# Input product: three weight slots converted again in the second token pair instead of being completed and stored in the first

## The chip, the cores and the metric

The kernel runs on one core of a Trainium2 chip. The metric is the device time of one execution in microseconds, the median of several executions. Engines are named as the profile names them: PE (TensorE matmuls) and PEld (its weight loads), DVE (VectorE), ACT (ScalarE), POOL (GpSimd) and SP (SyncE, which here does nothing but issue DMAs, one after the other).

## The reference

Three layers run one after the other on 3072 tokens of width 512: a chunked attention with eight memory rows, a feed-forward layer with `w_in` and `w_out`, and a gated feed-forward layer after an RMS norm.

```python
x = attention(q, k, v, mem_k, mem_v)        # (4, 8, 768, 64) -> (3072, 512)
h = x @ w_in                                # w_in (512, 2048)
sp = np.where(h > 20.0, h, np.log1p(np.exp(np.minimum(h, 20.0))))
x = (h * np.tanh(sp)) @ w_out
xn = x / np.sqrt(np.mean(x * x, axis=-1, keepdims=True) + 1e-06) * rms_g
g = xn @ w_gate
out = (g / (1 + np.exp(-g)) * (xn @ w_val)) @ w_out2
```

The weights come as 64-bit floats, so the kernel has to turn them into 32-bit ones on the chip before it can multiply with them. The change touches only `h = x @ w_in`.

## The kernel before

**Tokens.** The 3072 tokens are eight blocks of 384, taken as four token pairs j = 0 to 3. Before a pair can be multiplied, its two blocks have to come out of the attention, in pieces (`att_a` to `att_e1`) that are placed between the products of the pair before. The attention's inputs are loaded two tiles of 128 tokens ahead (`kn`, `qn`, and `vw` in eight small DMAs a tile).

**The input product.** `w_in` is cut into eight keys ("i", 0) to ("i", 7) of 256 columns. Every operand is a high and a low part, so a product is six matmuls of 384 columns (lines 566 to 568). The first pair is multiplied in the plain way: `unit(b, i)` takes block b and key i with four products, 16 units in all. The other three pairs use `group1(j, i)`, a scheme with seven products for both blocks, eight groups in each pair. Its token side needs seven sums of the pair's blocks (`t_pieces`, `sum_pieces`: lines 542 to 545, then six splits at lines 140 and 141, the last thing before a pair can run), its weight side seven pieces of a key. A group leaves its four PSUM banks by ACT copies and DVE additions (lines 577 to 598 and 653).

**Weight slots.** Five slots of 1792 KB (`W_SLOT` = 0, 4, 3, 2, 1, 0, 4, 3 for keys 0 to 7) hold the eight keys in turn: keys 5, 7 and 6 come into the slots of keys 0, 1 and 2.

**Conversion.** `cv_all` is one long sequence of steps which `cv_upto` moves on between products. A key has two raw halves of 512 KB, loaded into two raw buffers in turn (`load_raw`, line 136; a new load has to wait until line 188 has read the half before last). Each half takes ACT lines 180 and 183, then DVE lines 187, 188 and 194. A plain job (`add_plain`) then splits four pieces (lines 140 on ACT and 141 on DVE), which is what `unit` needs. A pair job (`add_pair`, used for the later weights) adds four sums (two on POOL, two on DVE) and splits all seven pieces. All of a conversion's instructions on ACT and most on DVE are pinned: they keep their program order.

**Completion.** `finish(key)` makes the seven pieces from the four of a plain job: two additions on DVE that rebuild the 32-bit weights (line 254), two sums on POOL (lines 259 and 260), two on DVE (lines 261 and 262) and two splits. In the first pair keys 0, 1, 2 and 7 are completed, in the second 6, 5, 4 and 3. A key that loses its slot is stored to device memory in two halves by `w_store` (line 124, `wi<-w`): keys 0, 1 and 2 in the first pair, 7, 6 and 5 in the second. `reload` brings a key back as one load (line 119, `w<-wi`): keys 2, 1, 0 in the second pair, 5, 6, 7 in the third, 2, 1, 0 in the fourth.

**What sets the order.** `slots` hands out the work between products: attention pieces, conversion steps, `finish` steps and stores at slot numbers. The instruction order on each engine is then fixed when the program is built. Each engine runs its own list in order, and all DMAs are in the one list of SP: an instruction that waits holds back all that stand behind it on its engine.

Of the kernel before, what the change touches and what calls it, by code (L numbers as in the profile page):

```python
# [24 lines left out]
W_AT = {1: 0, 2: 1, 4: 2, 3: 3, 5: 4, 6: 5, 7: 6}  # L25
W_IN = {1: 0, 2: 1, 3: 2, 4: 3, 5: 4, 6: 5, 7: 6}
# [3 lines left out]
def tile_kernel(  # L30
# [67 lines left out]
    def store_later(dst, src):  # L98
        late.append((tick[0] + 2, dst, src))

    def flush(all_=False):
        tick[0] += 1
        while late and (all_ or late[0][0] <= tick[0]):
            _, dst, src = late.pop(0)
            nc.sync.dma_start(out=dst, in_=src)
# [6 lines left out]
    wtab, wslot = {}, {}  # L112
# [4 lines left out]
    def w_load(key, u):  # L117
        s = w_slot(u)
        nc.sync.dma_start(out=s.bitcast(F32), in_=wd[key].bitcast(F32))
        wtab[key] = as7(s)  # L120
# [28 lines left out]
    def add_pair(key, arr0, f0, arr1, f1, u, keep, store):  # L149
        jobs.append(("pair", key, [(arr0, "col", f0), (arr1, "col", f1)], u, keep, store))  # L150

    def add_plain(key, arr, f0, f1, u):
        jobs.append(("plain", key, [(arr, "col", f0), (arr, "col", f1)], u, True, False))
# [4 lines left out]
    def add_rows(keys, arr, fs, u):  # L158
        jobs.append(("rows", keys, [(arr, "row", f) for f in fs], u, True, False))
# [111 lines left out]
    def cv_upto(n):  # L271
        while cv_n[0] < n:
            next(cv[0], None)
            cv_n[0] += 1

    def need(key):
        while key not in wtab:
            cv_upto(cv_n[0] + 1)
# [223 lines left out]
    def att_list(j):  # L502

        out = []
        t0 = TPP * j
        for s in range(TPP + 4):
            for op, lag in (("e", 4), ("d", 3), ("c", 2), ("b", 1), ("a", 0)):
                t = t0 + s - lag
                if t0 <= t < t0 + TPP:
                    if op == "a" and t % SPB == 0:  # L510
                        out.append([(att_a0, t)])
                    out.append([(att_ops[op], t), (att_ops[op + "1"], t)])
        return out
# [7 lines left out]
    def t_pieces(j, x0, x1, new, dram, tab):  # L521

        return sum_pieces(j, x0[:, 0:2, :], x0[:, 2:4, :], x1[:, 0:2, :], x1[:, 2:4, :],
                          new, dram, tab)
# [34 lines left out]
    def product(at, w, t, bank_, first):  # L559
        ws = w[:, at].rearrange("p l (k f) -> p l k f", k=2)  # L560
        ps = bank_[:, 0:N]
        for kk in range(2):
            whi, wlo = ws[:, 0, kk, :], ws[:, 1, kk, :]
            xh, xl = t[:, 0, kk, :], t[:, 1, kk, :]
            more = dict(skip_group_check=not first)
            nc.tensor.matmul(ps, whi, xh, start=first and kk == 0, stop=False, **more)  # L566
            nc.tensor.matmul(ps, whi, xl, start=False, stop=False, **more)  # L567
            nc.tensor.matmul(ps, wlo, xh, start=False, stop=kk == 1, **more)  # L568
# [41 lines left out]
    def unit(b, i):  # L610
        need(("i", i))
        w = wtab["i", i]
        g = gp.tile([128, 2, N], F32, tag="g", name="g")
        for e in range(2):
            ps = bk[(2 * n_unit[0] + e) % 4]
            for half in range(2):
                product(2 * e + half, w, xtab[b, half], ps, half == 0)
                if half:
                    nc.scalar.copy(g[:, e, :], ps[:, 0:N])
                    if e:  # L620
                        store_later(
                            g_d[0, 2 * i:2 * i + 2, :, b, :].rearrange("f p n -> p f n"), g
                        )
                yield
        n_unit[0] += 1

    def run(parts, between):
        while parts:
            for part in list(parts):
                if next(part, "end") == "end":  # L630
                    parts.remove(part)
                else:
                    between()
# [3 lines left out]
    def group_banks(of):  # L637
        g = n_group[0]
        n_group[0] += 1
        return [bk[(4 * g + i) % of] for i in range(4)]  # L640
# [4 lines left out]
    def group1_parts(j, i):  # L645
        need(("i", i))
        g = [gp.tile([128, 2, N], F32, tag="g", name="g") for _ in range(2)]
        ts = {p: ttab_x[j, p] for p in ORDER}
        mul = lambda p, bank_, first: product(W_IN[p], wtab["i", i], ts[p], bank_, first)
        banks = group_banks(4)  # L650
        c11 = banks[0][:, 0:N]
        yield from group(mul, banks, N, g[0][:, 1, :], g[1][:, 0, :], g[1][:, 1, :])
        nc.scalar.copy(g[0][:, 0, :], c11)
        for e in range(2):
            store_later(g_d[j, 2 * i + e], g[e])
# [21 lines left out]
    class Feed:  # L677
# [24 lines left out]
        def next(self, s):  # L702
            self.load(s + 3)
            self.split(s + 3)
            self.load(s + 5)
            return self.out.pop(0)
# [100 lines left out]
    W_SLOT = (0, 4, 3, 2, 1, 0, 4, 3)  # L807
    up = list(range(F1 // 2))
    down = up[::-1]
    for i in (0, 1, 2, 3, 4, 5, 7, 6):  # L810
        add_plain(("i", i), w_in, 2 * i, 2 * i + 1, W_SLOT[i])
    for f, u in zip(range(0, F1, 3), (5, 6, 7, 1, 2, 3)):
        fs = range(f, min(f + 3, F1))
        add_rows([("o1", x) for x in fs], w_out, fs, u)
# [16 lines left out]
    first = att_list(0)  # L831
# [25 lines left out]
    def slots(pieces, conv, tail=(), more={}, cap=10 ** 6):  # L857


        state = dict(n=0, att=0, tail=0)  # L860
        plist, n_slots = pieces
        first_cv, to = conv
        base = cv_n[0]

        def between():
            state["n"] += 1
            n = state["n"]
            flush()
            if n in more:
                more[n]()  # L870
            span = n_slots - 7
            while state["att"] < len(plist) and state["att"] * span < n * len(plist):
                for fn, t in plist[state["att"]]:
                    fn(t)
                state["att"] += 1
            if n > first_cv:
                cv_upto(min(cap, base + (to - base) * (n - first_cv) // (n_slots - first_cv)))
            if n >= n_slots - 7 and tail:
                if state["tail"] == 0:
                    state["t"] = tail()  # L880
                    for fn in state["t"][0]:
                        fn()
                elif state["tail"] <= len(state["t"][1]):
                    state["t"][1][state["tail"] - 1]()
                state["tail"] += 1

        return between

    def tail_of(j):
        return lambda: t_pieces(j, xb.pop(2 * j), xb.pop(2 * j + 1), t_new, None, ttab_x)  # L890

    def keep_w(i, half):
        return lambda: w_store(("i", i), half)

    def reload(pos, seq):
        if pos < 3:
            w_load(("i", seq[5 + pos]), W_SLOT[seq[5 + pos]])

    CV_I = 64

    def then(more, n, fn):
        more.setdefault(n, []).append(fn)

    def finish_at(more, i, n):
        part = finish(("i", i))
        for step in range(3):
            then(more, n + step, lambda: next(part))

    def calls(more):
        return {n: (lambda fns=fns: [fn() for fn in fns]) for n, fns in more.items()}  # L910
# [2 lines left out]
    units += [(b, i) for i in (2, 3, 4, 5, 7, 6) if i >= NHEAD for b in range(2)]  # L913
    at = {u: 4 * n + 4 for n, u in enumerate(units)}
    more = {}
    for i in range(3):
        finish_at(more, i, at[1, i] + 1)
        for half in range(2):
            then(more, at[1, i] + 4 + 3 * half, keep_w(i, half))
    finish_at(more, 7, at[1, 7] + 1)  # L920
    bt = slots((att_list(1), 4 * len(units)), (0, 73), tail_of(1), calls(more), CV_I)
    for b, i in units:
        run([unit(b, i)], bt)
    more = {}
    for i, ns in ((7, (3, 5)), (6, (9, 12)), (5, (16, 19))):
        for half, n in enumerate(ns):
            then(more, n, keep_w(i, half))
    for n, i in enumerate((6, 5, 4, 3)):
        finish_at(more, i, 7 * n + 1)
    bt = slots((att_list(2), 56), (0, 0), tail_of(2), calls(more))  # L930
    for pos, i in enumerate(down):
        group1(1, i, bt)
        reload(pos, down)
    bt = slots((att_list(3), 56), (0, 0), tail_of(3))
    for pos, i in enumerate(up):
        group1(2, i, bt)
        reload(pos, up)
    att_stack.close()
    w2p[0] = ctx.enter_context(
        tc.tile_pool(name="w2p", bufs=1, side="right", reuse_waits="tile")  # L940
    )
    bt = slots(([], 56), (0, CV_I + 64))
# [26 lines left out]
    for s, (m, i) in enumerate(steps):  # L969
# [3 lines left out]
        if i == F1 // 2 - 1 and m < NB - 1:  # L973
            assert not pend
            n = order[m]
# [54 lines left out]
    bt = between2(CV_I + 196, 140)  # L1030
# [29 lines left out]
    bt = between2(CV_I + 262, 125)  # L1060
# [53 lines left out]
```

## Time and profile before

| | us |
|---|---|
| median of 3 runs | 1208.36 (1205.7 to 1210.33) |
| profiled execution | 1208.05 |
| its span, first to last instruction | 1206.3 |
| PE busy | 1164.7 (97%) |
| DVE busy | 820.8 (68%) |
| ACT busy | 623.3 (52%) |
| POOL busy | 210.5 (17%) |

The stages of the input product in this execution: the units of the first pair run from 44.5 to 156.5 us, the groups of the second pair from 156.5 to 246, of the third to 328, of the fourth to 391. A share of 97% for PE is an average; the rows below are read by stage. Where a timeline is shown, a number in square brackets behind a row is the time for which the engine sat idle before it, with what ended that.

### The profile page before, as it was taken

To read this page: it belongs to the slowest core of one execution; us is meant where nothing else is said; L and a number is where in the kernel's file an instruction comes from. 1 tells how busy PE (TensorE), PEld (TensorE's weight loads), DVE (VectorE), ACT (ScalarE), POOL (GpSimd) and SP (SyncE) were. 2 spreads that over 40 slices of the span, in tenths; PEclk is the share of its full clock that TensorE was granted. 3 is DMA by queue.
4 is the path that set the end of the run, shared out by engine and by line. 5 is a ranking of instruction groups with operands and counts; after the bars stand their busy time and mean duration, and the time that the engine had idled before them with its cause. 6 is when DMAs were issued, how large, how long until landed. Compare 5 with 4: busy or idle time off the path is not lost.

```text
span 1206.3 us, 24873 instructions
## 1 busy us (share of the span) xinstructions
PE 1164.7 (97%) x9944; PEld 1128.4 (94%) x9944; DVE 820.8 (68%) x1331; ACT 623.3 (52%) x1055; POOL 210.5 (17%) x203
## 2 busy tenths in 40 slices
PE   5899889999999999999999999999999999999998
PEld 4788779888998999999999989999999999999998
DVE  3676695563676866668586876676667665987773
ACT  4565454343456874776866554443434433444442
POOL 2030131111134311111101222212122211100000
PEclk8799989999999999999999999999999999999999
DMA  9999889778387843858559788888397669755540
GB/s 184 207 260 268 223 253 295 206 215 248 104 345 268 294 146 121 324 176 300 192 179 410 289 335 341 321 331 332 109 356 276 267 223 337 190 161 141 141 132 36
DMA packets 216052, 287.50 MB, mean 238 GB/s; under 512 B 103552, under 2 KB 181376, under 8 KB 211712
## 3 DMA queue, kind: packets, MB, share of 16 engines
q1 hardware_dynamic: 215936, 285.91, 71.7%
q8 instruction: 78, 1.28, 0.4%
q14 instruction: 38, 0.31, 0.1%
HBM read 180.49 MB, written 105.38 MB: 237 GB/s over the span
## 4 chain that ended last, share of the span: by engine, by line
PE 81%; DMA 7%; DVE 6%; ACT 3%; issue 2%; SPq 1%; POOL 0%; DVEq 0%; ACTq 0%; POOLq 0%
PE bk L566 13%; PE bk L567 12%; PE bk L568 12%; PE bk L674 4%; PE bk L673 4%; PE bk L675 4%; PE bk L786 4%; PE bk L787 4%; PE bk L788 4%; DMA raw<-in_moe_w_in_dram 2%; PE bkp L566 2%; PE bkp L568 2%; PE bkp L567 2%; PE bkp L675 2%; PE bkp L674 2%; PE bkp L673 2%
## 5 line engine op out<-in xcount | busy, mean ns | idle before, releaser
L566 PE MATMUL bk<-T,w 128*128 128x384 f32 x992 | 340.3, 345 | 4.8 <-DMA T<-nt_scratch 1.8
L567 PE MATMUL bk<-T,w 128*128 128x384 f32 x992 | 335.1, 338 | 0.0
L568 PE MATMUL bk<-T,w 128*128 128x384 f32 x992 | 331.3, 337 | 0.1
L566 PEld LDWEIGHTS bk<-T,w 128*128 128x128 f32 x992 | 187.3, 189 | 10.6 <-DMA T<-nt_scratch 2.8
L567 PEld LDWEIGHTS bk<-T,w 128*128 128x128 f32 x992 | 187.7, 189 | 0.9
L568 PEld LDWEIGHTS bk<-T,w 128*128 128x128 f32 x992 | 186.9, 189 | 0.5 <-DVE w L141 0.4
L673 PE MATMUL bk<-T,w 128*128 128x384 f32 x384 | 130.6, 342 | 1.7 <-DVE s L593 1.7
L674 PE MATMUL bk<-T,w 128*128 128x384 f32 x384 | 129.9, 338 | 1.7 <-DVE T L141 1.7
L675 PE MATMUL bk<-T,w 128*128 128x384 f32 x384 | 129.4, 337 | 0.0
L786 PE MATMUL bk<-w,T 128*128 128x256 f32 x396 | 111.7, 282 | 0.0
L788 PE MATMUL bk<-w,T 128*128 128x256 f32 x396 | 111.4, 282 | 0.0
L787 PE MATMUL bk<-w,T 128*128 128x256 f32 x396 | 111.3, 281 | 0.0
L593 DVE TENSOR_TENSOR s<-bk,s 128x384 f32<-128x384 f32 (+1 forms) x84 | 45.0, 536 | 91.2 <-PE bk L568 81.7
L597 POOL TENSOR_TENSOR v<-s,z 128x384 f32<-128x384 f32 x48 | 53.2, 1109 | 193.5 <-DVE s L593 128.4
L141 DVE TENSOR_TENSOR T<-g,T 128x768 fp32r<-128x768 f32 x64 | 66.0, 1048 | 20.9 <-ACT T L140 20.8
L674 PEld LDWEIGHTS bk<-T,w 128*128 128x128 f32 x384 | 72.7, 189 | 3.1 <-DVE T L141 2.3
L787 PEld LDWEIGHTS bk<-w,T 128*128 128x128 f32 x396 | 75.5, 191 | 0.0
L673 PEld LDWEIGHTS bk<-T,w 128*128 128x128 f32 x384 | 72.6, 189 | 2.9 <-ACT ca L180 2.0
L786 PEld LDWEIGHTS bk<-w,T 128*128 128x128 f32 x396 | 75.2, 190 | 0.0
L141 DVE TENSOR_TENSOR T<-w,T 128x768 fp32r<-128x768 f32 x60 | 58.8, 991 | 23.9 <-ACT T L140 23.1
L788 PEld LDWEIGHTS bk<-w,T 128*128 128x128 f32 x396 | 75.1, 190 | 0.0
L140 ACT CAST T<-w 128x768 fp32r<-128x768 f32 x60 | 49.3, 833 | 47.5 <-PE bk L788 28.4
(158 smaller groups left out, 2358.1 us busy)
## 6 DMA issues: line engine op xcount, KB each, us to landing
T<-nt_scratch SPq DMA_DIRECT2D x49, 768.0 KB
g_scratch<-g SPq DMA_DIRECT2D x64, 384.0 KB
g<-g_scratch SPq DMA_DIRECT2D x64, 384.0 KB
h_scratch<-s SPq DMA_DIRECT2D x48, 384.0 KB
w<-h_scratch SPq DMA_DIRECT2D x24, 768.0 KB
w<-wi SPq DMA_DIRECT2D x9, 1792.0 KB
nt_scratch<-T SPq DMA_DIRECT2D x21, 768.0 KB
raw<-in_moe_w_out_dram SPq DMA_DIRECT2D x28, 512.0 KB
```

The lines of the kernel that those rows point to most:

```text
L140: keep(nc.scalar.copy(hi, src))
L141: keep((eng or nc.vector).tensor_tensor(lo, src, hi.bitcast(F32), op=ALU.subtract))
L566: nc.tensor.matmul(ps, whi, xh, start=first and kk == 0, stop=False, **more)
L567: nc.tensor.matmul(ps, whi, xl, start=False, stop=False, **more)
L568: nc.tensor.matmul(ps, wlo, xh, start=False, stop=kk == 1, **more)
L597: nc.gpsimd.tensor_tensor(c22, u3, z5, op=ALU.add)
L673: nc.tensor.matmul(ps, ahi, bhi, start=start, stop=False)
L674: nc.tensor.matmul(ps, ahi, blo, start=False, stop=False)
L675: nc.tensor.matmul(ps, alo, bhi, start=False, stop=stop)
L786: nc.tensor.matmul(ps, t[:, 0, f], w[:, 0], start=first and f == 0, stop=False, **more)
L787: nc.tensor.matmul(ps, t[:, 0, f], w[:, 1], start=False, stop=False, **more)
L788: nc.tensor.matmul(ps, t[:, 1, f], w[:, 0], start=False, stop=f == HG - 1, **more)
```

## The change

Keys 0, 1 and 2 are no longer completed and no longer stored in the first pair: their three `finish` calls and six `w_store` calls go. When the first pair is done the three entries are dropped from the table. The second pair no longer reloads them. Instead three pair jobs for keys 2, 1 and 0 stand behind the eight plain jobs in the conversion sequence: the raw columns are loaded again and converted in full, all seven pieces, one step in each slot from slot 13 to slot 45 of the second pair's 56. Their slots 3, 4 and 0 come free when groups 6, 7 and 5 of that pair are done. `add_pair` leaves its pieces in the order `W_AT`, so `group1` uses that order for keys below 3. The six half stores of these keys move to slots 1 to 17 of the third pair; the reload in the fourth pair stays. The `finish` steps of keys 6, 5, 4, 3 in the second pair move from slots 1, 8, 15, 22 to slots 1, 4, 7, 10.

```diff
-        mul = lambda p, bank_, first: product(W_IN[p], wtab["i", i], ts[p], bank_, first)
+        at = W_AT if i < 3 else W_IN
+        mul = lambda p, bank_, first: product(at[p], wtab["i", i], ts[p], bank_, first)
...
+    for i in (2, 1, 0):
+        add_pair(("i", i), w_in, 2 * i, w_in, 2 * i + 1, W_SLOT[i], True, False)
...
-    for i in range(3):
-        finish_at(more, i, at[1, i] + 1)
-        for half in range(2):
-            then(more, at[1, i] + 4 + 3 * half, keep_w(i, half))
...
+    for i in range(3):
+        del wtab["i", i]
...
-        finish_at(more, i, 7 * n + 1)
-    bt = slots((att_list(2), 56), (0, 0), tail_of(2), calls(more))
-    for pos, i in enumerate(down):
+        finish_at(more, i, 3 * n + 1)
+    for n, i in ((8, 2), (15, 1), (22, 0)):
+        then(more, n, lambda: None)
+    bt = slots((att_list(2), 56), (12, CV_I + 33 + 11), tail_of(2), calls(more), CV_I + 33)
+    for i in down:
         group1(1, i, bt)
-        reload(pos, down)
-    bt = slots((att_list(3), 56), (0, 0), tail_of(3))
+    more = {}
+    for i, ns in ((0, (1, 3)), (1, (8, 10)), (2, (15, 17))):
+        for half, n in enumerate(ns):
+            then(more, n, keep_w(i, half))
+    bt = slots((att_list(3), 56), (0, 0), tail_of(3), calls(more))
     for pos, i in enumerate(up):
         group1(2, i, bt)
         reload(pos, up)
+    CV_I += 33
```

The order of SP's DMAs in the first pair, before, around the raw halves of keys 5 and 7 (`raw`: a raw half; `wi<-w`: half a completed key to device memory; `vw`, `kn`, `qn`: attention inputs):

```order
L136 DMA raw<-in_moe_w_in_dram 128x4x256
L124 DMA wi<-w 128x1792
L335 DMA vw<-in_v_dram 56x4x64 x8
L124 DMA wi<-w 128x1792
L136 DMA raw<-in_moe_w_in_dram 128x4x256
L300 DMA kn<-in_mem_k_dram 8x8x64 x2
L301 DMA kn<-in_k_dram 112x8x64
L314 DMA qn<-in_q_dram 128x8x64
L105 DMA g_scratch<-g 128x2x384 x2
L136 DMA raw<-in_moe_w_in_dram 128x4x256
```

The same place now:

```order
L136 DMA raw<-in_moe_w_in_dram 128x4x256
L335 DMA vw<-in_v_dram 56x4x64 x8
L136 DMA raw<-in_moe_w_in_dram 128x4x256
L105 DMA g_scratch<-g 128x2x384
L314 DMA qn<-in_q_dram 128x8x64
L300 DMA kn<-in_mem_k_dram 8x8x64 x2
L301 DMA kn<-in_k_dram 112x8x64
L105 DMA g_scratch<-g 128x2x384
L136 DMA raw<-in_moe_w_in_dram 128x4x256
```

The stores between the raw halves are gone; the attention loads between them are the same ones.

DVE's order where the first pair ends, before: the completion of key 7, the start of the next (L254), the second pair's token sums (L542 to L545), and L360, a copy of attention keys.

```order
L141 TENSOR_TENSOR w<-ca,w 128x2x256
L254 TENSOR_TENSOR ca<-w 128x512
L261 TENSOR_TENSOR sm<-sm,ca 128x256
L262 TENSOR_TENSOR sm<-ca,sm 128x256
L254 TENSOR_TENSOR ca<-w 128x512
L365 COPY kw<-bk_90 128x4x32
L368 COPY kw<-bk_90 128x16x8
L254 TENSOR_TENSOR ca<-w 128x512
L542 TENSOR_TENSOR xb<-xb 128x768
L368 COPY kw<-kw 128x16x8
L141 TENSOR_TENSOR w<-sm,w 128x3x256
L141 TENSOR_TENSOR w<-sm,w 128x256
```

The same place now:

```order
L261 TENSOR_TENSOR sm<-sm,ca 128x256
L262 TENSOR_TENSOR sm<-ca,sm 128x256
L254 TENSOR_TENSOR ca<-w 128x512 x2
L141 TENSOR_TENSOR w<-sm,w 128x3x256
L365 COPY kw<-bk_90 128x4x32
L368 COPY kw<-bk_90 128x16x8
L141 TENSOR_TENSOR w<-sm,w 128x256
L542 TENSOR_TENSOR xb<-xb 128x768
L368 COPY kw<-kw 128x16x8
L543 TENSOR_TENSOR t<-xb 128x768
L545 TENSOR_TENSOR xb<-xb 128x768
L544 TENSOR_TENSOR t<-t,xb 128x768
```

Key 7's two splits moved ahead of the token sums, and the four sums now stand in one run.

DVE's order in the second pair's third group, before (L581 to L598 are a group's way out of PSUM, L141 with `w` the last split of a completion, the others attention):

```order
L581 TENSOR_TENSOR u_2656<-bk_86,s_2602 128x384
L141 TENSOR_TENSOR w<-sm,w 128x256
L428 TENSOR_REDUCE mx<-bkp 128x8
L365 COPY kw<-bk_90 128x4x32
L429 TENSOR_TENSOR p<-bkp,mx 128x2x4x64
L593 TENSOR_TENSOR s_2602<-bk_86,s_2602 128x384
```

The same place now (L187, L188 and L194 belong to the new conversions):

```order
L187 TENSOR_SCALAR ca<-ca 128x512
L188 SCALAR_TENSOR_TENSOR ca<-raw,ca 128x512
L141 TENSOR_TENSOR w<-sm,w 128x256
L581 TENSOR_TENSOR u_2633<-bk_86,s_2587 128x384
L428 TENSOR_REDUCE mx<-bkp 128x8
L360 COPY kw<-bk_90 128x4x24
L429 TENSOR_TENSOR p<-bkp,mx 128x2x4x64
L194 ISA ca<-ca,lr 128x1024
L365 COPY kw<-bk_90 128x4x32
L187 TENSOR_SCALAR ca<-ca 128x512
L593 TENSOR_TENSOR s_2587<-bk_86,s_2587 128x384
L188 SCALAR_TENSOR_TENSOR ca<-raw,ca 128x512
```

Steps of a conversion now stand between a group's additions.

## Rows read from the trace of the kernel before

**Rows 1.** Idle time of PE in its timeline, 117 to 232 us

```profile
119.64 0.66 PE L490 MATMUL bk<-ident,x 128*128 128x128 f32 x4 [1.67 <-ACT qT L405]
...
128.70 0.44 PE L566 MATMUL bk<-T,w 128*128 128x384 f32 x1 [0.76 <-ACT w L140]
...
135.29 0.65 PE L447 MATMUL bk<-ident,p 128*128 128x128 f32 x4 [0.97 <-DVE p L438]
...
137.52 0.79 PE L490 MATMUL bk<-ident,x 128*128 128x128 f32 x4 [1.57 <-DVE x L480]
...
155.70 0.89 PE L415 MATMUL bkp<-kw,qT 64*32 64x64 f32 x38 [3.81 <-DVE kw L360]
...
229.55 1.38 PE L464 MATMUL bkp<-vw,pT 64*32 64x65 f32 x12 [1.24 <-DMA vw<-in_v_dram]
```

**Rows 2.** Stretches: length; busy PE, PEld, DVE, ACT, POOL; PE clock, DMA share, GB/s

```profile
76.00:118.00 42.00, 41.97 (x669) 38.93 (x667) 28.98 (x58) 24.88 (x48) 3.38 (x4) 1.00 0.93 286
118.00:145.70 27.70, 22.55 (x362) 20.16 (x362) 16.64 (x32) 15.04 (x29) 1.19 (x2) 0.94 0.90 236
145.70:166.00 20.30, 16.25 (x152) 14.23 (x159) 18.99 (x28) 12.99 (x24) 7.28 (x7) 0.83 0.86 250
166.00:197.40 31.40, 31.40 (x481) 29.50 (x482) 24.87 (x51) 14.77 (x29) 7.67 (x9) 1.00 0.83 270
...
246.00:328.00 82.00, 80.57 (x1151) 73.99 (x1152) 42.77 (x84) 31.30 (x57) 8.57 (x8) 1.00 0.64 189
340.00:360.00 20.00, 20.00 (x117) 20.00 (x116) 14.26 (x24) 10.34 (x20) 9.02 (x7) 1.00 1.00 401
166.00:246.00 80.00, 78.04 (x1132) 71.55 (x1133) 50.34 (x98) 33.11 (x61) 15.67 (x17) 1.00 0.84 249
```

**Rows 3.** ACT: its wait for raw halves, 62 to 160 us: total, times, longest

```profile
ACT ca L180 <- DMA raw<-in_moe_w_in_dram: 15.5, 6, 5.7
```

**Rows 4.** ACT's timeline: the first raw half of key 6

```profile
132.80 0.66 ACT L180 ACTIVATE ca<-raw 128x512 f32<-128x512 f32 x1 [3.77 <-DMA raw<-in_moe_w_in_dram]
```

**Rows 5.** SP's timeline: start, time to issue, line, transfer, count

```profile
80.44 0.91 SPq L124 DMA_DIRECT2D wi<-w  x1
...
102.84 7.43 SPq L335 DMA_DIRECT2D vw<-in_v_dram  x8
110.33 1.04 SPq L124 DMA_DIRECT2D wi<-w  x1
111.47 0.40 SPq L136 DMA_DIRECT2D raw<-in_moe_w_in_dram  x1
...
126.88 0.79 SPq L136 DMA_DIRECT2D raw<-in_moe_w_in_dram  x1
...
128.31 5.89 SPq L335 DMA_DIRECT2D vw<-in_v_dram  x8
...
303.64 4.16 SPq L335 DMA_DIRECT2D vw<-in_v_dram  x8
```

**Rows 6.** DVE's timeline: first token sum, the copy behind the sums, last split

```profile
150.27 0.95 DVE L542 TENSOR_TENSOR xb<-xb 128x768 f32<-128x768 f32 x1
...
155.40 0.24 DVE L360 COPY kw<-bk 128x96 f32<-128x96 f32 x1
...
164.86 0.95 DVE L141 TENSOR_TENSOR T<-xb,T 128x768 fp32r<-128x768 f32 x1
```

**Rows 7.** Lines of a conversion and a completion, 40 to 520 us: ns min/median/max, first and last start

```profile
L187 DVE TENSOR_SCALAR ca<-ca x35: 350/420/1529, 42.3 to 514.3; 128x512 int32<-128x512 int32 x35
L188 DVE SCALAR_TENSOR_TENSOR ca<-raw,ca x35: 676/691/1675, 42.7 to 515.7; 128x512 int32<-128x512 int32 x35
L194 DVE CUSTOM_DVE_ANT_0 ca<-ca,lr x35: 676/693/1784, 43.5 to 516.4; 128x1024 uint16<-128x1024 uint16 x35
...
L254 DVE TENSOR_TENSOR ca<-w x16: 675/682/1325, 64.7 to 177.5; 128x512 f32<-128x512 f32 x16
L261 DVE TENSOR_TENSOR sm<-sm,ca x8: 416/934/957, 69.3 to 181.5; 128x256 f32<-128x256 f32 x8
```

## The prediction

> **What bounds the kernel now.** I read the busy shares by stretch first, then PE's idle time, then the engines that end it. On the whole PE is 97% busy, so a change beside PE can only win where PE is idle or slow. [rows 2] say where that is. From 76 to 118 us PE is busy for 41.97 of 42.00 at full clock: nothing to win there, however much is taken off the other engines. From 118 to 145.7 it is busy for 22.55 of 27.70, and its clock reads 0.94; from 145.7 to 166, where the first token pair ends and the second begins, 16.25 of 20.30 at 0.83. So the idle time is 5.15 and 4.05, and a clock that fell to its lower level (1.2 of 2.4 GHz) for part of these stretches costs up to 0.06 x 27.7 = 1.7 and 0.17 x 20.3 = 3.5. Together that is 14.4 us, and no more can come back in the first pair.
>
> What ends these waits? In the first stretch [rows 1] name ACT and DVE four times (1.67, 0.76, 0.97 and 1.57). But ACT is in that stretch busy for only 15.04 of 27.70: it runs its list in order, and at its head stands line 180, which waits for raw weights. Six times, for 15.5 in all, ACT sits before a raw half that has not landed [rows 3]; the attention copies behind it wait too, and PE waits for those. The first half of key 6 is issued at 126.88 [rows 5] and taken by ACT at 132.80, after 3.77 of idling [rows 4]. So the bound here is the chain of raw loads. In the second stretch it is DVE, busy for 18.99 of 20.30: PE waits 3.81 for a small copy [rows 1], L360, that starts at 155.40 behind three of the token sums, the first of which starts only at 150.27 [rows 6].
>
> **What the change takes off the first pair.** Three completions: on DVE two L254 of 0.68, two sums of 0.42 (the fastest L261) and splits of 0.42 and 0.95 each [rows 6, 7], 3.6 a key and 10.7 in all. They lie in the stretch before 118, where PE never waits, so by themselves they are worth nothing. The six stores matter more. They are 896 KB each, 5.5 MB, and stand between the raw halves on SP, from 80.44 to 110.33 [rows 5]. At the 286 GB/s of their own stretch that is 19 us of the DMA engines, at the 401 GB/s of 340 to 360 us, where the engines are at 1.00, 13.7 [rows 2]; they are at 0.93 while the stores run. The queue feels it: eight `vw` loads take SP 7.43 behind a store, 5.89 behind raw halves, 4.16 with little ahead [rows 5]. So a store costs its own issue (0.91 and 1.04 in the first and last of six) and about 1.5 in the loads behind it, 2.5 x 6 = 15, which agrees with 13.7. All of that stands ahead of the raw halves of keys 5, 7 and 6.
>
> The Trainium skill (Perfetto Trace Analysis, What "DMA-bound" means) says that a solid row of DMA slices on the issuing sequencer is descriptor generation and not data movement. By that only the six issue slices come free, some 5.5 us, the first term below would be 5.5 and the time 1202. The trace disagrees in part: the same eight loads have slices from 4.16 to 7.43, so the slices here also hold time that depends on the bytes ahead.
>
> **First term: the raw halves, 6.0 won.** PE would need the late halves some 6.9 earlier (5.15 of idle time and 1.7 of clock) to run through from 118 to 145.7. With 13.7 less ahead of them they can come that early. Against it: between the last three halves no store stood, only attention loads, so the shift has to be won by 111.47 and then merely kept, and stores of `g` that wait for ACT stay in the list. I take 6.0; the ends are 3.0 and 6.9.
>
> **Second term: the boundary of the pairs, 2.5 won.** This part of DVE's work hardly changes. The sums start 4.6 after PE's last attention transposes of the pair (145.7), although the ACT copy between takes under 1; the 3.8 over are DVE's backlog of conversions and key 7's completion. With earlier conversions part of it is done before. Key 7's two splits (0.95 and 0.42) now stand ahead of the sums. But L544, another 0.95 at least, now stands ahead of L360, for which PE waits, and then six token splits of 0.95 follow each other on DVE whatever PE does. The ends: 0 (the backlog stays and the two moves cancel) and 5.1 (3.8 and 1.3); the middle, 2.5.
>
> **Third term: DVE in the second pair, 1.7 lost.** A conversion costs DVE two halves of 0.42 + 0.69 + 0.69, two sums of 0.42, and splits of 0.68, 0.42, 0.68 and 0.68 (subtractions with two inputs, like L254) [rows 7]: 6.9, or 20.7 for three. From 166 to 246 DVE has 50.34 of 80.0; with 20.7 more it has 71, or 89%. That would fit, were it spread evenly. The 33 steps stand in slots 13 to 45, so 16 of them fall on groups 2 to 4 (slots 8 to 28): 10 us on top of 24.87 in 31.40, less up to 3 for completions that move ahead. DVE then needs 31.9 to 34.9 where PE takes 31.4: a loss of 0.5 to 3.5. It can be nothing as well, as PE had no idle time there at 79%. I take 1.7. ACT gets 24 casts and copies of at most 0.66 [rows 4], 16 us on 33.11 of 80, and stays off the bound.
>
> L261 has a fastest time of 0.416 and a median of 0.934 [rows 7]: behind a POOL sum it takes 0.52 more. The Trainium skill (SBUF — State Buffer, Who interferes with whom) speaks against the change here: a DVE instruction with two SBUF inputs and a GpSimd one that reads SBUF share a port, and the second fully blocks until the first ends. By it six POOL sums of the new conversions could hold DVE up for all of their own time in the second pair; by the row it is 3 x 0.52 = 1.6, less than the spread of the term, and so the sum stays.
>
> **Small terms.** The second pair loses three reloads of 1792 KB (5.5 MB) and gains raw loads of 3.1 MB. The one wait for a `vw` load there, 1.24 [rows 1], may go: 0.7 won (0 to 1.24). Four raw halves are requested within that pair and stand at ACT's head as before: 0.5 lost, up to 15 in a rival below. The six stores now add 13.7 to 19 us of DMA time to the third pair, at 0.64 of 82 us; 52 + 19 fits, but they come in its first third. Attention is loaded two tiles ahead, which covers them; without that cover a wait like the 1.24 appears: 0.5 lost (0 to 1.24). The DMAs of the reloads and all work of the fourth pair and after it keep their order: 0.
>
> **How the numbers follow.** 6.0 + 2.5 + 0.7 won, 1.7 + 0.5 + 0.5 lost: 6.5 won. Against the profiled execution's own 1208.05 us (span 1206.3; 0.3 below the median of the runs) that is 1201.5. A measurement of this kernel tells about 0.5% from no change, 6 us, so this is faster by barely more than that: 1202.3 divides the two.
>
> **Rivals.**
> - *DVE becomes the bound of the second pair.* For it: 89% on average, over 100% in groups 2 to 4, and an engine in order. Against: PE ran through at 79%. The third term is then 3.5 and the `vw` wait stays: 8.5 won, 4.5 lost, 1204.
> - *The room in the queue is filled by what stands behind.* SP's list between the last halves is the same as before, with waits for ACT and PE in it. The raw halves then come only 3 us earlier: 3.0 + 2.5 + 0.7 - 2.7 = 3.5 won, 1204.5.
> - *The raw waits move to the second pair (slower).* There PE's list has groups with four banks, and DVE has 9 us left. In the first pair 15.5 of waiting at ACT's head cost PE 14.4, nearly one for one. Four halves that each come as late as the one of [rows 4], 3.77, would cost 15.1 against the 8.5 won: 1214.7. From 2.1 each on, the gain is gone. Against it: fewer bytes in the pair, and the first two halves are asked for before it begins.
> - That the change does nothing can be left out: the stores are gone from SP's list and the conversions stand in DVE's.
>
> **Chances.** The forecast 0.55 (1199 to 1203.5, about four fifths of it below 1202.3), more than that 0.08 (both first terms at their upper ends, 1195 to 1199), DVE the bound 0.19, the queue filled 0.11, slower 0.07. So faster by over 0.5%: 0.55 x 0.8 + 0.08 and a little of the second rival, 0.55; within it 0.38; slower 0.07. The range goes from 1195, with the two first terms and the `vw` wait at their upper ends (6.9 + 5.1 + 1.2), to 1208, past both rivals of no change.
>
> **What would show it.** Right: ACT's total wait for raw halves in the first pair falls from 15.5 to under 6, PE's idle time from 118 us to the pair's end is gone but for 2 us, its clock stays at 1.00 there, and the second pair's first group ends some 8 us earlier, at about 158. First term wrong: the raw halves of key 6 still come after 130. Second: PE still waits over 3 for L360. Third: PE idles behind lines 581 to 598 in groups 2 to 4 for over 3 us, or not at all. A wait for `raw` at ACT's head in the second pair, or for `vw` in the third, would make it slower than said.

## The result

The changed kernel takes 1194.09 us (median of 6 runs, 1192.04 to 1198.16), the kernel before beside it 1210.36 (6 runs, 1205.7 to 1215.05). The ratio is 0.9895, with a 95% interval from 0.9866 to 0.9923: 9 to 16 us are won where 6.5 were forecast. It is faster, as said. The median lies one microsecond below the range's lower end of 1195; on the forecast's own base of 1208.05 the ratio gives 1195.4, just inside it. The profiled execution takes 1192.77 us, its span is 1191.0.

A first table places the gain. Both traces are cut at the same copies on ACT: the last copy of the first pair's own attention tokens, the copy that ends the first group of the second pair, and the eighth, sixteenth and last of the 24 groups. All times are us.

| stretch | before | after | won |
|---|---|---|---|
| ahead of the first cut (same work) | 61.6 | 60.5 | 1.1 |
| to the end of the second pair's first group | 104.3 | 93.8 | 10.5 |
| second pair, group 1 to 8 | 79.5 | 75.0 | 4.5 |
| third pair | 81.8 | 81.8 | 0.0 |
| fourth pair | 64.0 | 64.6 | -0.6 |
| the rest (same work) | 815.1 | 815.3 | -0.2 |

The 1.1 ahead of the first cut lies before anything that the change touches. The rest is the same work in every kernel below and takes 813.5 to 815.6 there, and the stretch ahead of the first cut 60.5 to 62.9: about 1 us either way in such a table is noise.

**The stretches of after**, which answer to [rows 2] (length; busy PE, PEld, DVE, ACT, POOL; PE clock, DMA share, GB/s):

```profile
118.00:140.00 22.00, 22.00 (x311) 20.95 (x310) 17.36 (x29) 11.68 (x22) 6.80 (x6) 1.00 0.72 179
140.00:154.40 14.40, 11.15 (x113) 8.98 (x112) 14.40 (x23) 9.56 (x18) 2.11 (x3) 0.88 0.93 287
154.40:229.40 75.00, 75.00 (x1106) 70.01 (x1105) 67.79 (x132) 43.49 (x82) 20.53 (x23) 1.00 0.80 230
229.40:311.10 81.70, 81.21 (x1183) 74.19 (x1183) 43.89 (x87) 33.52 (x60) 8.58 (x8) 1.00 0.82 264
```

From 118 to 140 PE no longer idles and its clock is at 1.00; before, the same part lost 5.15 of idle time and 1.7 of clock. At the pairs' boundary DVE is busy for 14.40 of 14.40, and PE still loses 3.25. In the second pair DVE is busy for 67.79 of 75.00, which is 90%, and PE for all of it.

**The raw halves of key 6 and, at 125.52, the first of key 2's second conversion**, in SP's timeline (start, time to issue):

```profile
113.11 1.15 SPq L136 DMA_DIRECT2D raw<-in_moe_w_in_dram  x1
...
116.19 4.93 SPq L335 DMA_DIRECT2D vw<-in_v_dram  x8
121.22 0.39 SPq L136 DMA_DIRECT2D raw<-in_moe_w_in_dram  x1
...
125.52 0.42 SPq L136 DMA_DIRECT2D raw<-in_moe_w_in_dram  x1
```

Key 6's first half is asked for at 113.11 instead of 126.88 [rows 5]. The last six halves of the first pair come 6.9 to 14.2 earlier (1.1 of it lies ahead of the first cut), and ACT's wait for raw halves, 15.5 us before [rows 3], is down to one of 0.3 in that stretch. PE's whole list of waits from 62 to 330 us is three rows (total, times, longest):

```profile
PE bk L566 <- ACT g L619: 3.0, 1, 3.0
PE bk L566 <- ACT g L654: 0.5, 1, 0.5
PE bk L351 <- DVE kw L368: 0.2, 1, 0.2
```

**What is late next** is still the boundary. DVE's timeline (start, duration):

```profile
141.59 0.94 DVE L542 TENSOR_TENSOR xb<-xb 128x768 f32<-128x768 f32 x1
142.46 0.74 DVE L368 COPY kw<-kw 128x128 f32<-128x128 f32 x1
143.12 1.49 DVE L543 TENSOR_TENSOR t<-xb 128x768 f32<-128x768 f32 x1
...
146.28 0.25 DVE L360 COPY kw<-bk 128x96 f32<-128x96 f32 x1
```

ACT's, with the idle time ahead of an instruction and what ended it:

```profile
144.65 0.83 ACT L140 CAST T<-t 128x768 fp32r<-128x768 f32 x1 [2.85 <-DVE t L543]
145.39 0.47 ACT L619 COPY g<-bk 128x384 f32<-128x384 f32 x1
```

And PE's:

```profile
145.91 0.44 PE L566 MATMUL bk<-T,w 128*128 128x384 f32 x1 [3.04 <-ACT g L619]
```

ACT's next cast waits 2.85 for a token sum of DVE; behind that cast, in ACT's list, stands the copy (L619) which empties the bank that PE wants. PE's wait of 3.04 is for that copy, not for the cast. L360, for which PE waited 3.81 before [rows 1], no longer stands in PE's list.

### The profile page after: what moved, and what is told of

It is laid out like the page before. It is cut to its first block, busy times and chain, and to the rows that moved or that the text cites. A ratio compares the mean times of both kernels' runs of the same rounds, so it can differ in the third digit from the quotient of the medians.

```text
span 1191.0 us, 24923 instructions
## 1 busy us (share of the span) xinstructions
PE 1157.4 (97%) x9944; PEld 1122.3 (94%) x9944; DVE 828.9 (70%) x1349; ACT 633.2 (53%) x1073; POOL 209.9 (18%) x203
## 4 chain that ended last, share of the span: by engine, by line
PE 81%; issue 6%; DMA 5%; DVE 4%; ACT 2%; SPq 1%; POOL 1%; DVEq 0%; ACTq 0%; POOLq 0%
PE bk L566 14%; PE bk L567 13%; PE bk L568 13%; PE bk L787 4%; PE bk L788 4%; PE bk L789 4%; PE bk L675 3%; PE bk L676 3%; PE bk L674 3%; PE bkp L566 2%; PE bkp L568 2%; PE bkp L567 2%; PE bkp L415 2%; PE bkp L676 1%; PE bkp L674 1%
## 5 line engine op out<-in xcount | busy, mean ns | idle before, releaser
L141 DVE TENSOR_TENSOR T<-g,T 128x768 fp32r<-128x768 f32 x64 | 65.9, 1047 | 21.2 <-ACT T L140 21.0
L141 DVE TENSOR_TENSOR T<-w,T 128x768 fp32r<-128x768 f32 x60 | 58.8, 991 | 23.7 <-ACT T L140 23.0
```

The lines of the kernel that those rows point to most:

```text
L141: keep((eng or nc.vector).tensor_tensor(lo, src, hi.bitcast(F32), op=ALU.subtract))
```

## The experiments

Each kernel is compared with the kernel before on its own chip. The table has the ratio with its 95% interval and, from the trace, the time to the end of the second pair's first group, the second pair, and pairs 2 to 4 together. The last column is the safest: in some kernels a piece of attention falls on the other side of a pair's end. It has a looseness of its own: the fourth pair takes 64.0 to 64.6 in most kernels, but 65.6 to 66.2 in four of them (no completions, before without reloads, more work on DVE, keys 5, 6, 7), where PE waits 1.2 to 1.4 more for one ACT copy. Of the kernel before, the second and third pair alone take 161.3; of the changed one, 156.8.

| kernel | ratio | first | second | pairs 2 to 4 |
|---|---|---|---|---|
| before | 1 | 104.3 | 79.5 | 225.3 |
| after | 0.9895 [0.9866, 0.9923] | 93.8 | 75.0 | 221.4 |
| no first-pair stores | 0.996 [0.9934, 0.9986] | 95.5 | 78.6 | 223.6 |
| no first-pair completions | 0.9994 [0.9971, 1.0017] | 106.0 | 80.8 | 228.3 |
| neither | 0.9918 [0.9882, 0.9954] | 94.5 | 76.3 | 221.9 |
| before without reloads | 0.9986 [0.9962, 1.001] | 103.4 | 74.3 | 221.6 |
| neither, without reloads | 0.9893 [0.9844, 0.9941] | 93.7 | 73.1 | 221.5 |
| before, completions early | 0.9972 [0.9946, 0.9997] | 104.9 | 78.3 | 223.4 |
| after with the reloads back | 0.9982 [0.9955, 1.0009] | 94.0 | 83.1 | 230.6 |
| after, no third-pair stores | 0.9875 [0.9841, 0.9909] | 94.5 | 74.5 | 220.1 |
| after with more work on DVE | 0.9951 [0.993, 0.9971] | 94.5 | 85.6 | 233.7 |
| keys 5, 6, 7 converted again too | 0.9893 [0.9857, 0.9929] | 94.0 | 73.3 | 221.6 |

**The first pair: stores or completions?** My theory was the stores in SP's list ahead of the raw halves, the rival DVE's completions.

No stores (the reloads read other stored keys):

```diff
...
     for i in range(3):
         finish_at(more, i, at[1, i] + 1)
-        for half in range(2):
-            then(more, at[1, i] + 4 + 3 * half, keep_w(i, half))
```

> The kernel before without its six stores of keys 0, 1, 2 in the first pair; the completions stay. The reloads of these keys in the second and fourth pair read keys 7, 6 and 5 from device memory instead (same bytes, other weights, so that part of h is not the reference's). Theory S (the room the stores take in SP's list and the DMA engines delays the raw halves): ACT's wait for raw halves in the first pair falls from 15.5 to under 3 us, the second pair's first group ends 9 to 11 us earlier than in the kernel before (165.9), the whole is about 1199. Rival C (the DVE and ACT time of the completions): ACT's wait stays over 10, the first group ends within 2 us of 165.9, 1209.

No completions (the stores stay, as many bytes, and write the first half twice):

```diff
...
     for i in range(3):
-        finish_at(more, i, at[1, i] + 1)
         for half in range(2):
```

> The kernel before without the three completions in the first pair; the six stores stay (the first half of each slot is stored twice, so pieces of keys 0, 1, 2 are wrong where they are reloaded). Theory S: ACT's wait for raw halves stays over 10 us, the first group ends within 3 us of 165.9, the whole 1207 to 1210. Rival C: the first group ends 8 to 11 us earlier, about 1199.

Neither, which takes both pieces out, with the reloads of the kernel without stores:

> The kernel before without the three completions and without the six stores; reloads of keys 0, 1, 2 read keys 7, 6, 5 (wrong weights there). Its first pair is that of the changed kernel, its second pair that of the kernel before. Theory R (the changed kernel won another 4 us in the second pair because the reloads are gone): first group ends at about 154 to 155, the second pair then takes 79 us from there, the whole is about 1198, 4 us over the changed kernel. Rival (the second pair gained by what was earlier in the first, not by the reloads): 75 us, 1194.

ACT's wait for raw halves from 62 to 160 us (total, times, longest), without the stores:

```profile
ACT ca L180 <- DMA raw<-in_moe_w_in_dram: 1.9, 1, 1.9
```

And without the completions, where line 181 is line 180 of the kernel before:

```profile
ACT ca L181 <- DMA raw<-in_moe_w_in_dram: 20.4, 6, 5.0
```

Without the stores the wait falls from 15.5 to 1.9 and the first pair ends 8.8 earlier; without the completions it is 20.4 and the pair ends no earlier. Both together give 9.8, nearly the 10.5 of the change. So in the profiled executions the stores carry the first pair; taking the completions away is worth nothing while the stores stand, and 1.0, which is the noise, once they are gone. The completions do move the raw halves, though: counted from the first cut, key 6's first half is asked for 9.9 earlier without the stores and 12.7 earlier without either. Less sure is the size over the whole kernel: the profiled run without stores lies near the fast end of its runs (1197.61 of 1196.42 to 1207.36), and by its ratio the stores alone are worth 1.7 to 8 us, where its span is 10.7 shorter. By the middles of the ratios the completions add 5 us to that (0.996 to 0.9918), but the intervals overlap; how much they add stays open. (The profiled run without completions, 1211.19, is the longest of its ten, whose median is 1206.14; its table row is at the high end.)

**The second pair: what gave 4.5?** The forecast had a loss there. First, the reloads taken out of the kernel before (its last three groups read the keys that still stand in the slots: 7, 6 and 5 in place of 2, 1 and 0):

```diff
         group1(1, i, bt)
-        reload(pos, down)
+        if pos < 3:
+            wtab["i", down[5 + pos]] = wtab["i", i]
```

> The kernel before, whose second pair does not reload keys 2, 1 and 0: its last three groups read the pieces of keys 7, 6 and 5, which still stand in those slots. Nothing else moves; the stores and completions of the first pair stay. Theory L (what the changed kernel won in the second pair, 79.5 to 75.0 us, came from the three loads of 1792 KB that are gone from SP's list): the second pair takes 75 to 76.5, PE no longer waits for vw there, and the time is some 3.5 us below the kernel before, ratio about 0.997. Rival (it came from the earlier completions, or from raw halves and stores that no longer trail into the pair): the second pair stays at 78.5 to 79.5, ratio 1.000.

The busy and idle time of the attention product that reads `vw`, over the second pair (count; busy, mean ns; idle ahead). In the kernel before:

```profile
L464 PE MATMUL bkp<-vw,pT 64*32 64x65 f32 x384 | 6.8, 225 | 1.4 <-DMA vw<-in_v_dram 1.4
```

In the changed kernel:

```profile
L464 PE MATMUL bkp<-vw,pT 64*32 64x65 f32 x384 | 5.2, 225 | 0.0
```

In the kernel before without the reloads:

```profile
L464 PE MATMUL bkp<-vw,pT 64*32 64x65 f32 x384 | 5.4, 225 | 0.0
```

The same 384 matmuls take 8.2 us before and 5.2 after: 1.4 of the difference is idle time, 1.6 is hidden in "busy", since matmuls that follow each other as eight small loads trickle in read as one busy stretch. It lies in one place, the block of 64 matmuls whose first 12 take 1.38 at 229.55 [rows 1]: that block takes 2.50 after its wait, a block that nothing holds up 0.86. Without the reloads nearly all of it is gone (5.4), and pairs 2 to 4 are 3.7 shorter (the second and third alone 5.7). Its stretch from 166 to 246 us, with the columns of [rows 2]:

```profile
166.00:246.00 80.00, 80.00 (x1127) 74.02 (x1126) 52.31 (x104) 35.16 (x64) 17.34 (x18) 1.00 0.69 198
```

PE is at 80.00 where it had 78.04 [rows 2]. The ratio of the runs (0.9986) is less sure than the trace, but its interval, from 4.6 us won to 1.2 lost, holds 3.7 and also nothing at all. Yet "neither" above keeps the reloads and also wins 3.4 in pairs 2 to 4: its second pair takes 76.3, where theory R, that the reloads alone made the difference, had 79. Both together:

> The kernel before without the completions and stores of keys 0, 1 and 2 in the first pair and without their reloads in the second, where the last three groups read keys 7, 6 and 5: what the changed kernel would be if its second conversions, its four spaced completions and its stores in the third pair cost nothing (the fourth pair loads other keys in place of 2, 1 and 0, as many bytes). If the second conversions are hidden altogether: as fast as the changed kernel, ratio 0.989, second pair 74.5 to 75.5. If they cost what the third term of the prediction says, 1.7 us: second pair 73.0 to 73.5, ratio 0.988. If they cost more, up to the rival's 3.5: 71.5, ratio 0.986.

It wins 3.8, not 7.1. The two are not additive: with either the reloads or the first pair's stores gone, PE waits little for `vw` any more (5.4 and 6.4 for its row, idle time included, beside 8.2). How the stores of the first pair reach into the second stays open: in "neither" SP still waits 6.9 us for reloads to land in the second pair, 6.8 in the kernel before. This kernel also prices the new conversions, since it is the changed kernel without them (and without the stores in the third pair, and with the completions of the second spaced as before): 221.5 beside 221.4 in pairs 2 to 4, 0.9893 beside 0.9895 in ratio. (Its second pair alone, 73.1, misleads: its third is 84.3, as a piece of attention went over the cut and PE idles there for 1.3; in both kernels PE is busy for the whole of the second pair.) Its second pair as a stretch:

```profile
154.90:228.00 73.10, 73.10 (x1096) 68.32 (x1096) 46.64 (x94) 31.21 (x58) 14.83 (x17) 1.00 0.67 198
```

So 21 us more on DVE (67.79 beside 46.64) cost PE nothing that can be told from the noise.

**Do the earlier completions matter?** In the kernel before, `7 * n + 1` becomes `3 * n + 1`.

> The kernel before with one part of the change alone: the completions of keys 6, 5, 4, 3 in the second pair at slots 1, 4, 7, 10 instead of 1, 8, 15, 22. If this part matters, the second pair is 2 us or more from 79.5 and the whole over 3 us from the kernel before; if it only makes room for the new conversions (my theory), both within 1 us.

The ratio is 0.9972; the first pair is unchanged (104.9), pairs 2 to 4 are 1.9 shorter, about twice the noise and more than the 1 us that was expected; the ratio's interval, too, is just clear of 1. It may give a little, but the second pair doesn't need it: the kernel "neither, without reloads" has its completions spaced as before and wins as much as the changed one. The changed kernel with its completions spaced as before wasn't tried.

**What if raw loads and reloads stand in one pair?** In the changed kernel the three 1792 KB loads come back into the second pair, into the slots to which they went, where nothing reads them:

```diff
...
-    for i in down:
+    for pos, i in enumerate(down):
         group1(1, i, bt)
+        if pos < 3:
+            s = w_slot(W_SLOT[i])
+            nc.sync.dma_start(out=s.bitcast(F32), in_=wd["i", i].bitcast(F32))
```

> The changed kernel with three loads of 1792 KB back in the second pair, after its first, second and third group, into the slots that the new conversions then overwrite; the output is the reference's. Theory R: the wait for vw loads near the seventh group comes back, the second pair takes 78 to 80 us from its first group's end instead of 75, the whole 1197 to 1199. Rival: within 1 us of the changed kernel, 1194.

All of the gain but 2 us is gone: 9.2 more in pairs 2 to 4, 10.5 by the ratios. The later part of its second pair, as a stretch:

```profile
190.70:240.00 49.30, 46.73 (x618) 41.63 (x615) 34.38 (x65) 22.20 (x44) 11.19 (x11) 0.97 0.94 273
```

And the row of the product that reads `vw`, over the pair:

```profile
L464 PE MATMUL bkp<-vw,pT 64*32 64x65 f32 x384 | 7.1, 225 | 1.6 <-DMA vw<-in_v_dram 1.6
```

The pair takes 83.1, more than the 78 to 80 of theory R. The DMA engines are at 0.94, as they were at 0.93 from 76 to 118 us before [rows 2]; PE idles for 2.57 and its clock falls to 0.97. The row of `vw` accounts for 3.5 of it (8.7 beside 5.2); the clock (0.03 of 49.3) for 1.5 at most; of the other 4, 0.9 is more idle time of PE in the second pair and 3.0 in the third (3.5 there beside 0.5 in the changed kernel). The raw halves are late again as well: in the second pair ACT waits for them three times, 7.1 in all, where it has no such wait in the changed kernel. One wait belongs to this experiment alone: ACT sits for 3.7 until a reload has landed in the slot that its next split overwrites. So the 9.2 is not the price of the queue alone.

**Do the stores cost anything in the third pair?** The changed kernel without them (the fourth pair reloads other keys):

```diff
...
-    for i, ns in ((0, (1, 3)), (1, (8, 10)), (2, (15, 17))):
-        for half, n in enumerate(ns):
-            then(more, n, keep_w(i, half))
```

> The changed kernel without the six stores in the third pair; the reloads of keys 2, 1, 0 in the fourth pair read keys 7, 6, 5 from device memory instead (wrong weights there, same bytes). Theory: the stores are hidden in the third pair, whose 81.8 us stay within 0.7, and the whole within 2 us of the changed kernel, 1194. Rival (they crowd the third pair as the reloads did the second): 78 to 80 us there, the whole 1190 to 1192.

The third pair takes 81.6 beside 81.8, and the ratio's interval (0.9841 to 0.9909) overlaps that of the changed kernel: within the noise they are hidden there, where they cost 8.8 in the first pair of the profiled execution.

**How much room has DVE left?** 33 products of 384 columns more on DVE, one in each slot from 13 to 45 of the second pair, with nothing that reads them (in place of three steps that do nothing):

```diff
-    for n, i in ((8, 2), (15, 1), (22, 0)):
-        then(more, n, lambda: None)
+    scr = sqp.tile([128, N], F32, tag="q", name="scr")
+    nc.vector.memset(scr, 1.0)
+    for n in range(13, 46):
+        then(more, n, lambda: pin(nc.vector.tensor_tensor(scr, scr, scr, op=ALU.mult)))
```

> The changed kernel with one more DVE product of 384 columns (0.5 to 0.6 us) in each of the slots 13 to 45 of the second pair, 33 in all, 16 to 18 us; the output is the reference's. DVE is busy for 67.8 of 75.0 us there without it. Theory (DVE has about 7 us left and no more; its load was next to be the bound): the second pair grows by 8 to 12 us to 83 to 87. Rival (PE waits only for transfers, DVE is far from the bound): under 3 us.

The products' own row on DVE (count; busy, mean ns; idle ahead):

```profile
L934 DVE TENSOR_TENSOR scr<-scr 128x384 f32<-128x384 f32 x33 | 20.0, 607 | 0.1
```

And the second pair as a stretch:

```profile
156.80:242.40 85.60, 79.58 (x1107) 71.79 (x1105) 82.90 (x166) 44.11 (x83) 21.64 (x23) 0.96 0.75 216
```

DVE's busy time rises by 15.1, from 67.79 to 82.90 (the products overlap their neighbours). The changed kernel left it 7.2; the pair grows by 10.6, of which 15.1 - 7.2 = 7.9 is work that no longer fits and 2.7 DVE's own waits. PE idles for 6.0 there, and every wait in its list for this pair, 5.9 in all, is for DVE; its clock is at 0.96. The profiled execution (1205.89) is the longest of its ten; by the ratios the loss is 6.8. So the rival "DVE becomes the bound" has a mechanism that sets in here once the room of 7 us is used up; the change alone does not reach it.

**Does the same trick pay once more?** In the third pair keys 5, 6 and 7 are converted again too, instead of being stored in the second and reloaded:

```diff
...
-    for i in (2, 1, 0):
+    for i in (2, 1, 0, 5, 6, 7):
         add_pair(("i", i), w_in, 2 * i, w_in, 2 * i + 1, W_SLOT[i], True, False)
...
-    for i, ns in ((7, (3, 5)), (6, (9, 12)), (5, (16, 19))):
...
         group1(2, i, bt)
-        reload(pos, up)
...
```

> The changed kernel with the same step for keys 5, 6 and 7: no stores of them in the second pair (5.5 MB less), no reloads in the third (5.5 MB less); they are converted again in full in slots 13 to 45 of the third pair (3.1 MB of raw columns, 20.7 us of DVE more). The output is the reference's. Theory (only room for transfers matters, and PE has no idle time left in the second pair): within 2 us of the changed kernel in the profile, 1192 to 1194, the third pair unchanged within 1 us at DVE about 80%. Rival (transfers still cost PE what the profile does not show as idle time): 3 to 6 us faster, 1188 to 1191.

0.9893 beside 0.9895: the same. PE had one wait of 0.5 left in these pairs, so taking bytes out of the queue there has next to nothing to win. No kernel tried beats the changed one by more than its interval.

## Why the prediction was right in direction and too small

- **What bounds the kernel: right.** The chain of raw loads behind the stores was the bound of the late first pair; in the profiled execution, taking the stores alone away moved its end by 8.8.
- **First term, 6.0: 6.9.** All of the 5.15 + 1.7 between 118 and 145.7 came back, the upper end. I held back because the last three halves have no store between them; but key 6's first half came 13.8 earlier, 12.7 counted from the first cut. That this is near the 13.7 worked out from the stores' bytes is in part luck: the stores alone moved it by 9.9, and the rest came once the completions went too, which the prediction had as worth nothing by themselves. The Trainium skill (Perfetto Trace Analysis, What "DMA-bound" means) calls slices like these descriptor generation. Read as the prediction read it, by issue slices alone, the stores would have freed 5.2 (the six slices added up); the 9.9 disagrees with reading it that way here.
- **Second term, 2.5: 2.6.** Idle time 4.05 and clock 3.5 at the boundary became 3.25 and 0.12 x 14.4 = 1.7: 7.55 less 4.95. The number is right by luck, for the way was not the one named: DVE's backlog stayed (the token sums start 4.3 after PE's last attention transposes of the pair, 4.6 before), L360 is out of PE's list, but the copy behind ACT's cast took its place, and more of the gain is clock (1.8) than idle time (0.8). That the first group would end at about 158 was too cautious by 4; "the idle time gone but for 2" left 3.25.
- **Small term of the `vw` wait, 0.7: 3.7. The step that failed most.** I took the one idle time of 1.24 as the end of the range. The line's whole row shows 3.0 of stall, 1.6 of it inside busy time, and the 3.7 is what the kernel before gains without its reloads; PE also had further small waits, as its list for the second and third pair of the kernel before shows (total, times, longest):

```profile
PE bkp L464 <- DMA vw<-in_v_dram: 1.4, 2, 1.2
PE bk L566 <- DVE g L596: 0.8, 1, 0.8
PE bkp L415 <- issue: 0.6, 1, 0.6
```

  In the kernel before without reloads none of the three is left. That the last two came from the queue as well is argued from that alone. Nor is the 3.7 the reloads' own: with the first pair's stores gone, taking the reloads away adds only 0.4 (221.9 to 221.5).
- **Third term, DVE, -1.7: 0.** DVE's load came out as forecast, 90% for 89%, and PE ran at 75.00 of 75.00, the "not at all" that the prediction had named as a sign against this term. The term set 31.9 to 34.9 of work on DVE in groups 2 to 4 against 31.4 of PE. DVE's work there came out as forecast, but PE's part of these groups is longer (502 matmuls for 481):

```profile
154.40:188.20 33.80, 33.80 (x502) 31.34 (x502) 32.67 (x67) 21.23 (x41) 9.25 (x11) 1.00 0.79 249
```

  So DVE kept up: 32.67 of 33.80 is 97%. Whether a lack in three groups would have been made good in those behind is not shown; that a loss comes when the whole pair is short, the run with more work on DVE shows. By the Trainium skill (SBUF — State Buffer, Who interferes with whom) a DVE instruction with two SBUF inputs and one on POOL that reads SBUF get in each other's way when they meet. The trace agrees: of the new conversions' instructions on DVE three ran beside a POOL sum, two splits (L141, 1.167 and 1.09 where the third took 0.682) and one sum (L235, 0.896 where the others took 0.411 and 0.417). That is 1.4 us together, near the prediction's 1.6, and PE lost nothing by it.
- **Raw waits in the second pair, -0.5: 0, and stores in the third, -0.5: 0.** ACT's list of waits has no `raw` in the second and third pair, and PE's no `vw`. The slower rival rested on halves as late as that of [rows 4]; its condition did not come, but it was near: with the reloads still in the list ACT waits 7.1 for raw halves, and the second pair is 8.1 longer. Its price was misread, though: it set all 14.4 against the 15.5 of waiting at ACT's head, of which only the 6.9 ahead of 145.7 belong to those waits.

The measured terms are 6.9 + 2.6 + 3.7 = 13.2, inside the interval's 9 to 16; the forecast's 6.5 lacks 0.9 + 0.1 + 3.0 + 1.7 + 0.5 + 0.5 of it. (The table of the result has 10.5 + 3.9 = 14.4 from the first cut on; the other 1.2 stands in no term.) Right in part for a reason not given: that the reloads go was costed as a single wait, while it also lets the raw loads in.

## What to carry to other kernels

Where one engine issues every DMA in order, price a transfer by the bytes that stand ahead of the next one that is waited for, stage by stage: the same six stores cost 8.8 us of the profiled execution ahead of the raw halves (1.7 to 8 by the runs) and nothing that can be told two pairs later. Read a late load from the whole row of the line that uses it, busy time beside idle time of a same count, for loads that trickle in can hide half of their stall in "busy", as here (1.6 of 3.0). And an engine beside the bound can have room up to a high share: here DVE went to 90% of a pair, and 97% of its first three groups, at no cost that can be told; count what is left (here 7 us) before adding the next thing.

## What the runs showed of the hardware

- SP takes longer over eight small `vw` loads where large transfers are ahead of them: 4.16 to 7.43 in [rows 5], and 10.4 to 10.6 at the three places behind a reload in the second pair (start, time to issue):

```profile
193.58 0.45 SPq L119 DMA_DIRECT2D w<-wi  x1
194.13 10.36 SPq L335 DMA_DIRECT2D vw<-in_v_dram  x8
```

  These times hold SP's own waits between the eight: of the 7.43, 1.9 is a wait until a store has landed, of the 10.36, 2.7 one for the reload; the eight issues by themselves add up to 4.6 and 6.4 there, 3.1 where the whole takes 4.16. SP's waits for large transfers to land, first in the first pair (40 to 160 us), then behind it (160 to 330), in the kernel before:

```profile
SPq L335 <- DMA wi<-w: 3.2, 2, 1.9
...
SPq L335 <- DMA w<-wi: 8.1, 3, 4.1
```

  Not every reload does it: behind those of the third pair the eight take 5.9 to 8.9.

- Two loads on the queue, the first pair's stores with their completions and the second pair's reloads, are worth 3.4 and 3.7 us in pairs 2 to 4 when taken away alone, and 3.8 together (3.4, 5.7 and 3.9 in the second and third pair).
- At the boundary the granted clock is 0.88 over 14.4 us, in a stretch in which PE idled for 3.25; in the stretch ahead of it, where PE never idles, it is 1.00.
